# Dealing the decode steps of the wide weights out anew among the experts

## The chip, the cores and the metric

One core of a Trainium2 chip. The metric is the device time of one execution in microseconds (us). Engines: PE (TensorE, matrix products), DVE (VectorE), ACT (ScalarE), POOL (GpSimd) and SP (SyncE, which issues nearly all loads here). A difference in time is judged against repeated runs of the same kernel.

## What is computed

A windowed attention (4 x 8 heads, 576 positions) gives 2304 tokens of 512 columns. A gate sends each token to one of eight experts. Then a wide layer follows, whose weights come as 64-bit floats:

```python
for e in range(8):                        # experts: w1[e] 512 x 1024, w2[e] 1024 x 512
    h = np.maximum(x[mask_e] @ w1[e], 0)
    out[mask_e] = gate_w[mask_e, None] * (h @ w2[e])
g = np.maximum(out @ w_in, 0) ** 2        # wide layer: w_in 512 x 2048, w_out 2048 x 512
return g @ w_out
```

## The kernel before, in words

**Stages.** Attention and routing come first, then the experts one after another, the fullest first, each with a fixed number of token columns (`ROWS`: 384, 384, 352, 352, 304, 256, 256, 224), then the wide layer in nine groups of 256 tokens. Rows that do not fit an expert's columns would be done in a loop under a branch (`overflow`, line 1053), which all engines pass after expert 7.

**An expert** (line 999). The first product, s1 (line 784), goes over eight blocks `fc` of 128 hidden columns: twelve matmuls into a PSUM bank (two names, two buffers each), then a relu whose high half is written by ACT (line 793) and whose low half, the rest to 32-bit precision, by DVE (line 794). The second, s2 (line 835), goes over four blocks `d`; each takes all eight `fc` in order, with lines 844 (high weight, high relu), 845 (high weight, low relu) and 846, and ACT copies the bank to `yT` (line 847). So s2 of an expert starts with the relu halves that s1 made, in the same order.

**Expert weights.** Four quarters of w1 and four of w2 per expert, 512 KB each. `raw_w` (line 737) loads one with a DMA of SP into a staging buffer, and `split` (line 762) turns it into two 16-bit halves, the high one on ACT (line 764), the low one on DVE (line 765), in a ring `wr` of twelve buffers. The quarters of expert e+1 are loaded and split by code that stands in expert e: those of w1 after `fc` 1, 3, 5 and 7, those of w2 after each `d`. `stage` (line 748) chooses the staging buffer: the raw ring `rw` of four buffers (`raw()`, line 123), or a tile of `wi_s` that the wide weights do not yet use, by the table `SPARE` (line 51).

**Decode steps.** The wide weights have to be turned from 64-bit floats into 32-bit ones and split. This is done in 32 steps, in this order (line 939): eight `out_step` (line 900; their result is sent to device memory and fetched again late), sixteen `in_step` (line 869), which fill the eight tiles `wi_s[0..7]`, two each, and eight `out_step` whose result is kept. A step loads into a buffer of the raw ring (lines 855 to 859), decodes on DVE with three operations into the one buffer `dec` (lines 864 to 866); an `in_step` then forms four sums (lines 887 to 890). Its finish is a high half on ACT (line 895, or 911) and a low half on DVE (line 896, or 912). A call of `wide()` (line 920) finishes the step of the call before and begins the next one. Six calls stand in front of expert 0; `STEPS` (line 49) lists for each expert after which `fc` of s1 and after which `d` of s2 a call stands; three more are in `moe2` (line 1230), behind the branch.

```python
STEPS = (((2, 6), ()), ((1, 5), (1,)), ((4,), (1,)), ...        # line 49
            if fc in STEPS[e][0]:                               # line 1019
                wide()
            if d in STEPS[e][1]:                                # line 1034, in then(d), called after each d of s2
                wide()
```

The wide layer's first products are `wide1` (line 1163), from `wi_s`, its second ones `wide2` (line 1199), from `wo_s`: `wide1(0, 0)` stands ahead of s2 of expert 7, `wide1(0, 1)` behind the branch, and `wide2(0, 0)`, which reads all eight kept tiles, after it. `norm` (line 1095) prepares a group's input; the first one runs in expert 6.

**Order.** The instructions of an engine run in one line, each waiting for its inputs and for the buffer it writes. That line is not the order of the code: instructions are ordered when the program is built, with the code's order as one input, so work can stand well ahead of where it is written if its buffers are free. SP's loads are one such line.

Of the kernel before, what the change touches and what calls it, by code (L numbers as in the profile page):

```python
# [45 lines left out]
TINY, HUGE = 1e-30, 1e30  # L46
GT = 2
GW = GT * P
STEPS = (((2, 6), ()), ((1, 5), (1,)), ((4,), (1,)), ((1, 5), (1,)), ((1, 5), (1,)), ((3,), (1, 3)), ((3,), (1, 3)),
         ((1, 3, 5, 7), (1, 3)))  # L50
SPARE = ((), (4, 5, 6, 7), (4, 5, 6, 7), (4, 5, 6, 7), (4, 5, 6, 7), (6, 7), (7,), ())
KEPT = (0, 1, 8, 9, 2, 3, 10, 11)
SENT = (4, 5, 12, 13, 6, 7, 14, 15)

# [35 lines left out]
class K:  # L90
# [656 lines left out]

    def stage(self, which, e, c):

        free = SPARE[e]  # L750
        n = 4 * (which - 1) + c
        if n % 2 == 0 and e > 1 or not free or (which, e) == (1, 1):
            return self.raw()
        return self.wi_s[free[(n if e == 1 else n // 2) % len(free)]].rearrange("p k a c -> p (k a c)").bitcast(F32)[:, :1024]

# [164 lines left out]
    def wide(self, k=1):  # L920
        def store():
            while len(self.stored) > (2 if self.steps and self.steps[0][0] != self.in_step else 0):
                self.stored.pop(0)()

        for _ in range(k):
            store()
            if self.finish:
                self.finish()
                self.finish = None
            if self.steps:  # L930
                f, *a = self.steps.pop(0)
                self.finish = f(*a)
# [22 lines left out]
    def experts(self, stack):  # L955
# [20 lines left out]
        def gather(e):  # L976
            c0, c1 = blocks(e)[0][0], blocks(e)[-1][0] + 1
            nc.gpsimd.tensor_scalar(idx[:, e, c0:c1], idt[:, e, c0:c1, 0], float(N - 1), None, op0=ALU.min)
            xgs[e] = [self.gather_x(idx[:m, e, c:c + 1]) for c, m in blocks(e)]
# [19 lines left out]
        for e in range(E):  # L999
# [10 lines left out]
            for fc in range(8):  # L1010
# [6 lines left out]
                if fc % 2 == 1 and more and e > 0:  # L1017
                    w[1, e + 1, fc // 2] = self.load_w(1, e + 1, fc // 2)
                if fc in STEPS[e][0]:
                    wide()  # L1020
# [5 lines left out]
            def then(d):  # L1026
                if more:
                    w[2, e + 1, d] = self.load_w(2, e + 1, d)
                if e + 2 < E:
                    if d == 0:  # L1030
                        prep(e + 2)
                    if d == 2:
                        gather(e + 2)
                if d in STEPS[e][1]:
                    wide()
# [280 lines left out]
```

## Time and profile before

| | |
|---|---|
| median of 3 runs | 775.46 us (773.32 to 777.34) |
| the profiled execution | 774.25 us |
| its span (first to last instruction) | 772.2 us |
| PE busy / weight loads busy | 728.1 us (94%) / 559.2 us (72%) |
| DVE / ACT / POOL busy | 540.1 us (70%) / 361.2 us (47%) / 133.7 us (17%) |
| mean granted TensorE clock | 0.984 of full speed |
| DMA | 91.63 MB |

The shares are averages over stages that differ: attention fills the first 170 us or so, the experts run to 413.6 us, and the wide layer, a long stretch of matmuls, takes the rest. What the change touches lies between 180 and 437 us, and is to be read there.

### The profile page before, as it was taken

To read this page: it belongs to the slowest core of one execution; us is meant where nothing else is said; L and a number is where in the kernel's file an instruction comes from. 1 tells how busy PE (TensorE), PEld (TensorE's weight loads), DVE (VectorE), ACT (ScalarE), POOL (GpSimd) and SP (SyncE) were. 2 spreads that over 40 slices of the span, in tenths; PEclk is the share of its full clock that TensorE was granted. 3 is DMA by queue.
4 is the path that set the end of the run, shared out by engine and by line. 5 is a ranking of instruction groups with operands and counts; after the bars stand their busy time and mean duration, and the time that the engine had idled before them with its cause. 6 is when DMAs were issued, how large, how long until landed. Compare 5 with 4: busy or idle time off the path is not lost. (4 is left out here: it accounts for less than half of the span.)

```text
span 772.2 us, 18404 instructions
## 1 busy us (share of the span) xinstructions
PE 728.1 (94%) x7547; PEld 559.2 (72%) x7547; DVE 540.1 (70%) x1352; ACT 361.2 (47%) x636; POOL 133.7 (17%) x183
## 2 busy tenths in 40 slices
PE   6989999998989899899798999999999999999996
PEld 5889899787646566688698777777777777777772
DVE  5898788855879897568798774747474756566440
ACT  5878898744556574465444342423232323323220
POOL 4583421525543020000000010101010000000001
PEclk9999999899999999999899999999999999999999
DMA  9796214867897874457514000000000000000000
GB/s 336 291 388 149 67 56 120 240 177 213 286 311 231 272 252 136 152 171 249 181 57 138 3 28 2 29 1 29 2 22 8 15 15 15 15 14 15 15 14 28
DMA packets 35650, 91.63 MB, mean 119 GB/s; under 512 B 5209, under 2 KB 13547, under 8 KB 35547
## 3 DMA queue, kind: packets, MB, share of 16 engines
q1 hardware_dynamic: 29803, 75.77, 30.3%
q0 software_dynamic: 5760, 14.65, 5.7%
q8 instruction: 61, 1.00, 0.5%
q14 instruction: 26, 0.21, 0.1%
HBM read 77.54 MB, written 13.04 MB: 117 GB/s over the span
## 5 line engine op out<-in xcount | busy, mean ns | idle before, releaser
L1159 PEld LDWEIGHTS <-wi 128*128 128x128 f16 x3024 | 170.4, 98 | 6.4 <-issue 2.6
L1220 POOL DMA_INDIRECT out_dram<-o,oid x18 | 17.5, 973 | 464.5 <-ACT o L1218 464.5
L1179 ACT CAST wr<-work 128x1024 f16<-128x1024 f32 x36 | 37.6, 1045 | 123.1 <-DVE work L1178 123.1
L845 PE MATMUL ps_c<-work,wr 128*128 128x352 f16 (+5 forms) x256 | 73.8, 294 | 10.2 <-DVE work L794 9.4
L844 PE MATMUL ps_c<-work,wr 128*128 128x352 f16 (+5 forms) x256 | 73.5, 293 | 5.9 <-ACT work L793 3.2
L846 PE MATMUL ps_c<-work,wr 128*128 128x352 f16 (+5 forms) x256 | 73.9, 294 | 0.0
L305 PE MATMUL ps_a<-yT,wr 128*128 128x192 f32 (+2 forms) x288 | 64.3, 343 | 6.6 <-DMA wr<-in_q_dram 5.0
L1184 DVE TENSOR_TENSOR work<-work 128x512 f32<-128x512 f32 x18 | 12.4, 692 | 77.2 <-ACT work L1171 77.2
L1159 PE MATMUL ps_c<-work,wi 128*128 128x128 f16 x1032 | 64.9, 219 | 0.0
L1159 PE MATMUL ps_a<-work,wi 128*128 128x128 f16 x1032 | 64.7, 219 | 0.0
L317 ACT ACTIVATE pb<-pb,nm 128x192 f32<-128x192 f32 (+2 forms) x144 | 56.2, 433 | 12.4 <-DVE nm L310 11.7
L1159 PE MATMUL ps_b<-work,wi 128*128 128x128 f16 x960 | 60.1, 219 | 1.5 <-DVEq L1057 1.5
L1211 PE MATMUL ps_d<-wr 128*128 128x512 f16 x144 | 54.6, 379 | 0.1
L1212 PE MATMUL ps_d<-wr 128*128 128x512 f16 x144 | 54.6, 379 | 0.0
L1213 PE MATMUL ps_d<-wr 128*128 128x512 f16 x144 | 54.6, 379 | 0.0
L1213 PE MATMUL ps_d<-rw,wr 128*128 128x512 f16 x144 | 54.6, 379 | 0.0
L1212 PE MATMUL ps_d<-rw,wr 128*128 128x512 f16 x144 | 54.6, 379 | 0.0
L1211 PE MATMUL ps_d<-rw,wr 128*128 128x512 f16 x144 | 54.6, 379 | 0.0
L1213 PEld LDWEIGHTS <-wr 128*128 128x128 f16 x288 | 28.1, 98 | 33.9
L765 DVE SCALAR_TENSOR_TENSOR wr<-rw,wr 128x1024 f16<-128x1024 f32 x36 | 43.7, 1217 | 11.1 <-ACT wr L764 11.0
L1180 DVE TENSOR_TENSOR wr<-work,wr 128x1024 f16<-128x1024 f32 x36 | 44.0, 1221 | 10.0 <-ACT wr L1179 10.0
L305 PEld LDWEIGHTS ps_a<-yT,wr 128*128 128x128 f32 x288 | 45.1, 199 | 7.8 <-DMA yT<-in_k_dram 6.1
(248 smaller groups left out, 1693.8 us busy)
## 6 DMA issues: line engine op xcount, KB each, us to landing
rw<-in_w_dram SPq DMA_DIRECT2D x36, 512.0 KB, 5.5
wi<-in_w_dram SPq DMA_DIRECT2D x24, 512.0 KB, 5.3
rw<-in_wo_dram SPq DMA_DIRECT2D x16, 512.0 KB, 4.2
rw<-in_wi_dram SPq DMA_DIRECT2D x32, 256.0 KB, 5.2
wr<-in_q_dram SPq DMA_DIRECT2D x14, 512.0 KB, 8.0
xd<-xhl POOLq DMA_DIRECT2D x16, 256.0 KB, 4.5
yT<-in_k_dram SPq DMA_DIRECT2D x7, 576.0 KB, 10.7
rw<-in_v_dram SPq DMA_DIRECT2D x12, 325.0 KB, 5.6
```

Of the source, the lines that this page charges most:

```text
L305: nc.tensor.matmul(ps[:, s, first:hi], q[g, u, hh // 4][:, hh % 4, s if u < 4 else 0, :], self.kt[g, hh // 2][:, hh % 2, key0:key0 + hi - ...
L317: self.last_exp = nc.scalar.activation(pb[:, s, first:hi], pb[:, s, first:hi], AF.Exp, bias=nm[:, s:s + 1], scale=-1.0)
L765: self.nc.vector.scalar_tensor_tensor(t[:, 1], st, sc, t[:, 0], op0=ALU.mult, op1=ALU.subtract)
L844: nc.tensor.matmul(py, wh, hh, start=fc == 0, stop=False)
L845: nc.tensor.matmul(py, wh, hl, start=False, stop=False)
L846: self.last_mm = nc.tensor.matmul(py, wl, hh, start=False, stop=fc == 7)
L1159: self.nc.tensor.matmul(ps[:, j], w[:, kp, a, w0 * P:(w0 + 1) * P], v[:, 2 * x + kp], start=kp + b == 0, stop=kp == 1 and b == 2)
L1179: nc.scalar.copy(g[0][:, :, i], ci)
L1180: V.tensor_tensor(g[1][:, :, i], ci, g[0][:, :, i], op=ALU.subtract)
L1211: nc.tensor.matmul(py, gh, wh, start=n == 0, stop=False)
L1212: nc.tensor.matmul(py, gh, wl, start=False, stop=False)
L1213: nc.tensor.matmul(py, gl, wh, start=False, stop=n == 15)
```

## The change

The table `STEPS` is dealt out anew, and `SPARE` is replaced by a count: a tile `wi_s[k]` may stage an expert's weights as long as no more than 2k - 2 in_steps have been begun by the code so far.

```diff
-STEPS = (((2, 6), ()), ((1, 5), (1,)), ((4,), (1,)), ((1, 5), (1,)), ((1, 5), (1,)), ((3,), (1, 3)), ((3,), (1, 3)),
+STEPS = (((1, 4, 6), ()), ((1, 5), (0, 2)), ((5,), (0, 2)), ((1, 5), (0, 2)), ((3,), (0, 2)), ((), (1,)), ((), ()),
          ((1, 3, 5, 7), (1, 3)))
-SPARE = ((), (4, 5, 6, 7), (4, 5, 6, 7), (4, 5, 6, 7), (4, 5, 6, 7), (6, 7), (7,), ())
...
     def stage(self, which, e, c):

-        free = SPARE[e]
+        begun = 16 - sum(f == self.in_step for f, *_ in self.steps) if e > 0 and (which, e) != (1, 1) else 16
+        free = [k for k in range(4, 8) if begun + 2 <= 2 * k]
         n = 4 * (which - 1) + c
-        if n % 2 == 0 and e > 1 or not free or (which, e) == (1, 1):
+        if n % 2 == 0 and e > 1 or not free:
             return self.raw()
```

Calls of `wide()` in experts 0 to 7: before 2, 3, 2, 3, 3, 3, 3, 6; after 3, 4, 3, 4, 3, 1, 0, 6.

## Rows read from the trace of the kernel before

**Rows 1.** Windows, experts 1 to 6: us; PE, PEld, DVE, ACT, POOL busy; clock; DMA.

```profile
198.92:235.98 37.06, 34.60 (x220) 20.56 (x217) 29.90 (x50) 20.10 (x31) 17.09 (x23) 0.95 0.88 296
235.98:268.38 32.40, 30.36 (x218) 19.97 (x216) 30.06 (x67) 18.37 (x27) 8.04 (x7) 1.00 0.78 254
268.38:299.23 30.85, 30.26 (x218) 19.81 (x216) 27.96 (x49) 19.28 (x30) 4.35 (x3) 1.00 0.75 237
299.23:331.80 32.57, 28.09 (x211) 20.45 (x209) 20.59 (x33) 16.45 (x26) 0.00 (x0) 0.95 0.35 114
331.80:354.77 22.97, 22.13 (x211) 19.64 (x208) 18.45 (x32) 13.82 (x23) 0.00 (x0) 1.00 0.77 249
354.77:385.90 31.13, 26.22 (x224) 21.41 (x222) 24.22 (x45) 15.92 (x26) 0.00 (x0) 0.89 0.59 190
```

**Rows 2.** Waits of PE from 198.92 to 413.61: us in total, times, longest.

```profile
PE ps_c L845 <- DVE work L794: 9.4, 13, 1.6
PE ps_c L844 <- ACT work L793: 3.2, 3, 2.1
```

**Rows 3.** Timeline of PE in expert 6: start, us, instruction [idle before, releaser].

```profile
372.25 0.27 PE L844 MATMUL ps_c<-work,wr 128*128 128x256 f16 x1 [2.08 <-ACT work L793]
...
374.78 0.37 PE L845 MATMUL ps_c<-work,wr 128*128 128x256 f16 x1 [1.27 <-DVE work L794]
```

**Rows 4.** Window within expert 6, columns as in rows 1.

```profile
372.50:378.00 5.50, 4.04 (x20) 2.62 (x19) 4.43 (x10) 3.19 (x4) 0.00 (x0) 0.51 0.65 191
```

**Rows 5.** Timeline of ACT in expert 6.

```profile
370.18 1.06 ACT L764 ACTIVATE wr<-rw 128x1024 f16<-128x1024 f32 x1 [2.21 <-DMA rw<-in_w_dram]
...
371.82 0.39 ACT L793 ACTIVATE work<-ps_a 128x256 f16<-128x256 f32 x1
```

**Rows 6.** DVE's groups by line, whole span: busy us, mean ns, idle before.

```profile
L865 DVE SCALAR_TENSOR_TENSOR dec<-rw,dec 128x512 uint32<-128x512 uint32 x32 | 22.1, 689 | 0.5
...
L896 DVE SCALAR_TENSOR_TENSOR wi<-dec,wi 128x896 f16<-128x896 f32 x16 | 17.4, 1086 | 7.8 <-ACT wi L895 7.8
...
L864 DVE TENSOR_SCALAR dec<-rw 128x512 uint32<-128x512 uint32 x32 | 13.6, 424 | 15.9 <-PE ps_c L846 7.9 <-DMA rw<-in_wi_dram 5.3 <-DMA rw<-in_wo_dram 2.2
...
L912 DVE SCALAR_TENSOR_TENSOR wi<-dec,wi 128x512 f16<-128x512 f32 x8 | 5.5, 692 | 3.5 <-ACT wi L911 3.5
...
L889 DVE TENSOR_TENSOR dec<-dec 128x128 f32<-128x128 f32 x16 | 4.5, 283 | 0.0
```

**Rows 7.** Timeline of DVE: the tenth and the sixteenth finish of an in_step.

```profile
297.69 1.09 DVE L896 SCALAR_TENSOR_TENSOR wi<-dec,wi 128x896 f16<-128x896 f32 x1 [1.02 <-ACT wi L895]
...
377.74 1.09 DVE L896 SCALAR_TENSOR_TENSOR wi<-dec,wi 128x896 f16<-128x896 f32 x1 [1.07 <-ACT wi L895]
```

**Rows 8.** DMA issues of the page: count, KB each, median us to landing.

```profile
rw<-in_w_dram SPq DMA_DIRECT2D x36, 512.0 KB, 5.5
wi<-in_w_dram SPq DMA_DIRECT2D x24, 512.0 KB, 5.3
```

**Rows 9.** Timeline of DVE in expert 4.

```profile
306.26 1.22 DVE L765 SCALAR_TENSOR_TENSOR wr<-wi,wr 128x1024 f16<-128x1024 f32 x1
...
315.55 0.43 DVE L864 TENSOR_SCALAR dec<-rw 128x512 uint32<-128x512 uint32 x1 [2.16 <-DMA rw<-in_wi_dram]
...
330.76 1.23 DVE L765 SCALAR_TENSOR_TENSOR wr<-rw,wr 128x1024 f16<-128x1024 f32 x1 [8.11 <-ACT wr L764]
```

**Rows 10.** Timeline at the branch: DVE's last decode before it, PE's first matmul after it.

```profile
414.14 0.69 DVE L866 SCALAR_TENSOR_TENSOR dec<-rw,dec 128x512 uint32<-128x512 uint32 x1
...
415.44 0.66 PE L1159 MATMUL ps_b<-work,wi 128*128 128x128 f16 x9 [1.45 <-DVEq L1057]
```

**Rows 11.** Timeline behind the branch: DVE's last kept tile, PE's next two matmuls of wide2.

```profile
422.54 0.67 DVE L912 SCALAR_TENSOR_TENSOR wr<-dec,wr 128x512 f16<-128x512 f32 x1
...
426.55 0.39 PE L1212 MATMUL ps_d<-wr 128*128 128x512 f16 x1
426.77 0.38 PE L1213 MATMUL ps_d<-wr 128*128 128x512 f16 x1
```

## The prediction

> **What bounds the kernel now.** I read the busy times by expert first, then TensorE's waits, then the instructions around the longest wait. Every expert is one stage: a first product (s1), a second (s2), on PE without a break unless an input is late. [rows 1] has the stages of experts 1 to 6. The column to read is length less PE busy: 37.06 - 34.60 = 2.46 us of idle PE in expert 1, then 2.04, 0.59, 4.48, 0.84, and 31.13 - 26.22 = 4.91 in expert 6 (up to the last s2 matmul). The second column is the granted clock: 0.95, 1.00, 1.00, 0.95, 1.00, 0.89. Where it is under 1.00, PE ran at the lower of its two levels (1.2 instead of 2.4 GHz) for a part of the stage, and length x (1 - clock) bounds what that took: 1.9 us in expert 1, 1.6 in expert 4, 3.4 in expert 6. In expert 6 the clock was low during a wait of 1.27 us too [rows 3], where half of that (0.6) cost nothing, so I count 2.8 there. A stretch of that stage shows the level itself, 0.51 [rows 4].
>
> PE's waits [rows 2] say for what: s2 waits 9.4 us for line 794 (DVE's half of the relu split, the low part of ht) and 3.2 us for line 793 (ACT's half); the two groups left, 2.8 us, are s1 waiting for line 794. No wait names a weight. So in these stages PE is late only when DVE or ACT has something else in its line ahead of the relu split. In all, experts 1 to 6 lose 15.3 us idle and about 6.3 us to the clock.
>
> The worst place is expert 6: the matmul at 372.25 waited 2.08 us for ACT, the one at 374.78 another 1.27 us for DVE [rows 3]. What stood in ACT's line is in [rows 5]: a weight split of expert 7 that waited 2.21 us for its DMA, then a transpose copy, and only then the relu at 371.82.
>
> **The decode steps.** One in_step costs DVE 0.42 + 0.69 + 0.69 for the three decode operations (L865 is as long as L866), 4 x 0.28 for L887 to L890 and 1.09 for L896: 4.0 us; one out_step 0.42 + 0.69 + 0.69 + 0.69 = 2.5 us [rows 6]. The sixteen L896 tell where the in_steps really ended: 2 in expert 1, 4 in expert 2, 4 in expert 3, 2 each in experts 4, 5 and 6 ([rows 7] has the tenth and the last). That is not where their calls stand: the tenth, done at 297.69, is closed by a call in s2 of expert 4, a stage that begins only at 299.23. The order on an engine is thus not that of the code; a call bounds its step only loosely, and steps ran early wherever buffers let them.
>
> **The change part by part.** Calls made by the end of experts 0 to 7 go from 8, 11, 13, 16, 19, 22, 25, 31 to 9, 13, 16, 20, 23, 24, 24, 30. The number of instructions and of DMAs stays; a step that moves takes its loads on SP's line with it.
>
> *Out of experts 5 and 6.* Before, four in_steps end there, 4 x 4.0 = 16 us of DVE, and the first kept out_step, 2.5 us. After, only in_step 16 is begun there (15 may end there). They also stop taking buffers of the raw ring: each took one of the four between expert 7's loads. DVE was busy 24.22 of 31.13 us in expert 6 [rows 1]; without some 10 us it has half its time free. Bounds: nothing returns, if the waiting weight split of [rows 5] is all that matters, or all of 4.9 + 2.8 = 7.7 us. I take all but 1.5 us (about twice the 0.84 of expert 5, which has as many rows and runs at full clock; the norm's operations stay in expert 6): **-6.2 us**. Expert 5 itself I leave, between -0.8 and +2.1 (one ACT wait as in [rows 3]).
>
> *Into experts 0 to 4.* By the end of expert 3 the calls are 20 instead of 16, but before the change the steps were already at the tenth in_step, which is call 19's work. So really moved into experts 1 to 3 is about one in_step, and two or three into expert 4. In expert 4 DVE is idle 32.57 - 20.59 = 12.0 us, 8.11 us of it in one piece that waits for a weight split [rows 9]: three steps of 4.0 fit. Its own loss (4.5 + 1.6 = 6.1 us) comes from four weight splits in a row (the last begins at 306.26) and from a decode that waited 2.16 us for its DMA ahead of a relu split [rows 9], and both can stay; bounds -6.1 and +4.0 (a step in front of the relu split). I take 0. In experts 1 to 3 DVE is idle 7.2, 2.3 and 2.9 us. If that covers the step, the cost is 0; if the step stands before s2, it is 4.0 and a drop of the clock as in expert 1, 1.9. I take one more stall of expert 2's size: **+2.0 us**. Expert 0's third call is within that: its step needs the one decode buffer, which the steps before it hold.
>
> Here a rule speaks against the change. What the rows show is that DVE's busy share does not foretell the stalls: it is 0.93 and 0.91 in experts 2 and 3, which lose 2.6 us together, and 0.78 in expert 6, which loses 4.9 [rows 1]. The Trainium skill (Perfetto Trace Analysis, Identifying the Most-Contended Engine) takes occupancy as the measure for the Vector engine and says to relieve the engine where it is highest; by it, steps would be moved into the two fullest stages. An estimate by that page: a step of 4.0 us against idle time of which little can be used, so about 4 us instead of my 2.0, and 2 us less gain. Stalls and busy share do not go together in this trace; where the rule holds, the third rival decides.
>
> *Staging.* Which weights are staged in wide-weight tiles changes: 24 loads go through wi and 36 through rw before [rows 8]; by the new rule 4 + 4 + 4 + 4 + 1 = 17 through wi, and 43 through rw. Loads take as long either way (5.3 and 5.5 us). For experts 5 to 7 SP then has four buffers alone. One buffer turns round in 5.5 (landing) + 1.06 (ACT's split) + 1.22 (DVE's) = 7.8 us [rows 5, 8, 9], so eight loads take 2 x 7.8 = 15.6 us, under expert 5's 22.97. Cost 0, hidden under s1 and s2; without that cover it is the 2.2 us of [rows 5] again, in experts 5 and 6: bounds 0 and +4.4. In expert 4, three loads and one of expert 5 share tile 7 on SP's in-order queue; before, expert 6's four did the same. 0. POOL's queue has no part in the change.
>
> *Expert 7 and the branch.* PE waits 1.45 us at the overflow branch for DVE, which decodes kept step 7 until 414.83 [rows 10]. After, the calls before the branch reach kept step 6 only, one out_step (2.5 us) less if in_step 16 is done early, as the others were: **-1.45 us** (bounds -1.45 and 0).
>
> *After the branch.* Two kept steps are loaded and decoded there instead of one. Before, the last one was ready at 422.54 + 0.67, and wide2 starts at 426.55 [rows 11]; it reads that tile as the last of eight, after 21 matmuls 0.22 us apart, 4.6 us later. One more step, 2.5 us, fits into 426.55 + 4.6 - 423.2 = 8.0 us. 0, and +2.5 without that cover.
>
> Sum: -6.2 + 2.0 - 1.45 = -5.65 us. The profiled execution took 774.25 us (span 772.2 and 2.05 around it), 1.21 under the median of 775.46, so I apply the difference to the median: **769.8 us**, -0.7%.
>
> **The rivals.** A difference under 0.5%, 3.9 us, is about what a measurement of this kernel cannot tell from none: 771.6 to 779.3.
>
> *Nothing much moves.* Steps run ahead of their calls already, and what held ACT in expert 6 was a late weight load, of which there are now more on four buffers. Then expert 6 keeps its 7.7 us: 775.46 + 2.0 - 1.45 = 776.0. For it: [rows 5, 7]. Against: two in_steps sat in the ring between just those loads.
>
> *Expert 4 clears too.* If decode steps earlier in the line leave its relu splits free, 6.1 us more: 769.8 - 6.1 = 763.7. For it: 12 us of idle DVE there. Against: the four weight splits in a row remain.
>
> *Slower: the early experts overflow.* Place: the turn from s1 to s2 in experts 1 to 3, where DVE is busy 0.81 to 0.93. Price: a step ahead of the relu split there holds PE 4.0 us, and about 1.9 us of low clock follows. The gain to eat is 6.2 + 1.45 = 7.65, so it decides from 7.65 + 3.9 = 11.5 us on: two steps and their clock, 11.8, are just enough; with three steps and two drops, 12.0 + 3.8 = 15.8, it is 775.46 - 7.65 + 15.8 = 783.6. For it: DVE has 5.2 us free in experts 2 and 3. Against: only about one step more really goes there. [rows 9] show the form it takes: a decode at the head of DVE's line with a relu split behind it.
>
> **How the numbers follow.** Forecast 0.42, expert 4 clears too 0.14, nothing moves 0.26, slower 0.18. So faster 0.56, same 0.26, slower 0.18. The forecast's own range is 766.3 (no rest in expert 6 and no early stall, 3.5 less) to 771.6. For 8 in 10 the range runs from 762.0 (the second rival and 1.7 below) to 780.0 (all of the no-change case and the edge of the slow one); about 0.15, mostly the slow case's, is left out.
>
> **What would show it.** Right: at most two L896 after expert 4's end, 17 and 43 loads on wi and rw, expert 6 with under 2 us of PE idle and a clock above 0.97, no wait at the branch. Wrong: expert 6 still waiting on lines 793 and 794, with ACT held by a weight load (first rival), or PE idle in experts 1 to 3 above 9 us (third).

## The result and the profile after

The changed kernel takes 780.55 us (776.25 to 784.30), the kernel before, on the same chip, 775.72: a ratio of **1.0071** [1.0053, 1.0089], 5.5 us slower by the ratio (4.8 by the medians) where 5.65 us of gain were forecast, and 0.55 us above the range that was to hold 8 times in 10. Profiled, its span is 777.1 us against 772.2.

The windows of the changed kernel, experts 1 to 6, columns as in [rows 1]:

```profile
198.47:236.91 38.44, 34.79 (x219) 20.42 (x217) 29.65 (x50) 20.10 (x30) 17.17 (x24) 0.96 0.84 267
236.91:273.63 36.72, 31.59 (x218) 20.49 (x216) 33.20 (x74) 19.59 (x28) 7.40 (x7) 0.95 0.75 243
273.63:309.78 36.15, 32.42 (x219) 20.49 (x217) 29.53 (x52) 20.43 (x31) 2.81 (x3) 0.95 0.65 204
309.78:339.98 30.20, 27.65 (x211) 20.25 (x209) 25.49 (x46) 15.78 (x25) 0.00 (x0) 0.94 0.62 191
339.98:367.60 27.62, 24.20 (x211) 20.53 (x209) 16.52 (x26) 15.54 (x25) 0.00 (x0) 0.94 0.54 174
367.60:391.68 24.08, 22.89 (x224) 20.26 (x222) 16.44 (x28) 13.22 (x23) 0.00 (x0) 1.00 0.57 198
```

Read the first column against [rows 1]: +1.38, +4.32, +5.30, -2.37, +4.65, -7.05 us. The last is the gain that was forecast (24.08 - 22.89 = 1.19 us idle, clock 1.00). Stages 2 and 3 lost most beside stage 5: idle PE (length less busy) went from 2.04 and 0.59 to 5.13 and 3.73, and the granted clock from 1.00 to 0.95. Stage 5, which was to stay, lost as much: its idle went from 0.84 to 3.42.

The waits of PE over the same stretch, to set beside [rows 2]:

```profile
PE ps_c L845 <- DVE work L794: 11.1, 11, 2.1
PE ps_a L790 <- DVE work L794: 4.4, 1, 4.4
PE ps_c L844 <- ACT work L793: 2.7, 3, 1.3
PE ps_b L790 <- DVE work L794: 1.3, 2, 0.7
```

The same lines 793 and 794, with one new long wait: a first matmul of s1 that stood 4.4 us. Nothing is left at the branch, where PE had waited 1.45 us [rows 10]. The loads are 17 through `wi` and 43 through `rw`, as counted.

**Stage 2: where the 4.4 us come from.** First ACT, then DVE, then PE, of the changed kernel:

```profile
239.77 1.06 ACT L764 ACTIVATE wr<-rw 128x1024 f16<-128x1024 f32 x1 [3.37 <-DMA rw<-in_w_dram]
...
245.39 1.06 ACT L764 ACTIVATE wr<-rw 128x1024 f16<-128x1024 f32 x1 [1.99 <-DMA rw<-in_w_dram]
246.35 0.45 ACT L793 ACTIVATE work<-ps_a 128x352 f16<-128x352 f32 x1
```

```profile
234.28 1.23 DVE L765 SCALAR_TENSOR_TENSOR wr<-rw,wr 128x1024 f16<-128x1024 f32 x1 [0.23 <-ACT wr L764]
...
244.88 0.41 DVE L864 TENSOR_SCALAR dec<-rw 128x512 uint32<-128x512 uint32 x1
...
248.74 0.52 DVE L794 SCALAR_TENSOR_TENSOR work<-ps_a,work 128x352 f16<-128x352 f32 x1
...
251.71 1.09 DVE L896 SCALAR_TENSOR_TENSOR wi<-dec,wi 128x896 f16<-128x896 f32 x1 [2.21 <-ACT wi L895]
```

```profile
238.55 0.31 PE L792 MATMUL ps_a<-work,wr 128*128 128x352 f16 x1
...
249.31 0.31 PE L790 MATMUL ps_a<-work,wr 128*128 128x352 f16 x1 [4.40 <-DVE work L794]
```

The late relu belongs to the first product of s1, which was done by 238.86 (238.55 + 0.31); PE makes three more products and then needs that bank again. ACT's half stood behind two weight splits that waited 3.37 and 1.99 us for their loads, so it began at 246.35. DVE's half came only at 248.74: no instruction of DVE's line between 234.28 and 251.71 had idle time before it, so from 234.28 on DVE worked off two decode steps, weight splits and small operations of the routing (lines 686 to 706), and the relu came behind them. Both lines were late. By ACT's half alone DVE could have begun at 246.80 and PE would have waited about 2.5 us; DVE's line held it for the full 4.40. DVE had also lost time earlier to late splits. Its waits for ACT's half of a split, from 198 to 275 us, before and after:

```profile
DVE wr L765 <- ACT wr L764: 3.7, 3, 2.2
```

```profile
DVE wr L765 <- ACT wr L764: 7.3, 6, 2.3
```

Its waits of all kinds grew less: up to this relu, from 198 to 249 us, they are 9.1 us against 8.1 before. So most of what stood ahead of the relu in DVE's line was its own work. The waits of ACT for the loads, from 195 to 400 us, before and then after:

```profile
ACT wr L764 <- DMA rw<-in_w_dram: 15.5, 10, 3.3
ACT wr L764 <- DMA wi<-in_w_dram: 9.9, 7, 2.1
```

```profile
ACT wr L764 <- DMA rw<-in_w_dram: 29.0, 16, 3.9
ACT wr L764 <- DMA wi<-in_w_dram: 16.4, 7, 3.8
```

From 25.4 to 45.4 us: in the changed kernel ACT waits nearly twice as long for weights, and a relu can stand behind a waiting split in ACT's and DVE's lines.

**Stage 5: the raw ring alone.** DVE and PE of the changed kernel:

```profile
340.45 4.63 DVE L765 SCALAR_TENSOR_TENSOR wr<-rw,wr 128x1024 f16<-128x1024 f32 x4 [0.16 <-ACT wr L764]
...
356.37 1.09 DVE L896 SCALAR_TENSOR_TENSOR wi<-dec,wi 128x896 f16<-128x896 f32 x1 [1.01 <-ACT wi L895]
357.38 0.42 DVE L794 SCALAR_TENSOR_TENSOR work<-ps_b,work 128x256 f16<-128x256 f32 x1
```

```profile
355.21 0.27 PE L845 MATMUL ps_c<-work,wr 128*128 128x256 f16 x1 [1.30 <-DVE work L794]
356.66 0.27 PE L844 MATMUL ps_c<-work,wr 128*128 128x256 f16 x1 [1.07 <-ACT work L793]
357.85 0.27 PE L845 MATMUL ps_c<-work,wr 128*128 128x256 f16 x1 [0.92 <-DVE work L794]
```

Four splits in a row (4.63 us) open the stage. The loads of three quarters of w1 of expert 6 were issued at 328.14, 331.40 and 332.01, and that of the fourth at 337.09, when a decode step had left its buffer; so w1 filled all four raw buffers. Their splits need room in the ring `wr`, which the last block `d` of s2 of expert 4 (336.9 to 340.1) gives up buffer by buffer, and the first load of w2 was issued at 341.70, behind the first of these splits. ACT then waits for those too:

```profile
345.55 1.06 ACT L764 ACTIVATE wr<-rw 128x1024 f16<-128x1024 f32 x1 [1.44 <-DMA rw<-in_w_dram]
...
351.35 1.06 ACT L764 ACTIVATE wr<-rw 128x1024 f16<-128x1024 f32 x1 [1.25 <-DMA rw<-in_w_dram]
```

By the time s2 begins, the finish of an in_step (356.37) stands ahead of the last relu, and PE waits 1.30 + 1.07 + 0.92 = 3.29 us of the stage's 3.42.

### The profile page after: what moved, and what is told of

Read it like the earlier page. It is cut to its first block, busy times and chain, and to the rows that moved or that the text cites. A ratio compares the mean times of both kernels' runs of the same rounds, so it can differ in the third digit from the quotient of the medians.

```text
span 777.1 us, 18408 instructions
## 1 busy us (share of the span) xinstructions
PE 729.9 (94%) x7547; PEld 558.9 (72%) x7547; DVE 538.3 (69%) x1352; ACT 360.9 (46%) x636; POOL 132.4 (17%) x183
## 5 line engine op out<-in xcount | busy, mean ns | idle before, releaser
L765 DVE SCALAR_TENSOR_TENSOR wr<-rw,wr 128x1024 f16<-128x1024 f32 x43 | 52.1, 1221 | 15.9 <-ACT wr L764 15.8
L764 ACT ACTIVATE wr<-rw 128x1024 f16<-128x1024 f32 x43 | 44.9, 1055 | 29.2 <-DMA rw<-in_w_dram 29.0
L1213 PEld LDWEIGHTS <-wr 128*128 128x128 f16 x288 | 28.2, 98 | 33.9
L309 DVE CUSTOM_DVE_ANT_0 pb<-ps_a,bias 128x192 f32<-128x192 f32 (+2 forms) x144 | 44.2, 327 | 9.7 <-PE ps_a L304 7.9
```

Source lines behind the costliest of these rows:

```text
L309: self.last_ttr = nc.vector.tensor_tensor_reduce(out=pb[:, s, first:hi], in0=ps[:, s, first:hi], in1=self.bias[:, hh, first - lo:192], sca ...
L764: self.nc.scalar.activation(t[:, 0], st, AF.Copy, scale=sc)
L765: self.nc.vector.scalar_tensor_tensor(t[:, 1], st, sc, t[:, 0], op0=ALU.mult, op1=ALU.subtract)
L1213: nc.tensor.matmul(py, gl, wh, start=False, stop=n == 15)
```

## The experiments

Two theories, which do not exclude each other. **A: late loads in an in-order line.** Weight loads come late, for want of staging buffers (tile 7 shared by expert 4's loads, the raw ring alone for experts 5 to 7) and behind the moved steps' loads; their splits wait at the head of ACT's and DVE's lines, and the relu behind them. **B: DVE is full.** The moved decode work itself fills DVE in experts 1 to 3. Ratios are to the kernel before, run beside each kernel on the same chip; it took 775.72 us beside the change, 770.66 beside 1 to 4, 774.60 beside 5 to 8 and 770.80 beside 9 to 12, so kernels are compared by ratio. In the profiled executions expert 0 ends at 195.1, 199.3 and 196.1 us in the mean of these three groups, so most of that difference lies ahead of the stages. The stage lengths of the profiled executions, experts 1 to 6, in us:

| kernel | ratio [95%] | 1 | 2 | 3 | 4 | 5 | 6 |
|---|---|---|---|---|---|---|---|
| before | 1 | 37.1 | 32.4 | 30.9 | 32.6 | 23.0 | 31.1 |
| after | 1.0071 [1.0053, 1.0089] | 38.4 | 36.7 | 36.2 | 30.2 | 27.6 | 24.1 |
| after, again (x5) | 1.0063 [1.0037, 1.0089] | 37.2 | 36.3 | 33.9 | 32.5 | 28.6 | 25.9 |
| long staging (x1) | 1.0011 [0.9988, 1.0034] | 39.8 | 34.6 | 31.8 | 30.9 | 23.4 | 24.5 |
| staging rule alone (x2) | 0.9973 [0.9947, 0.9999] | 34.7 | 34.4 | 29.9 | 30.7 | 23.0 | 26.8 |
| late move only (x3) | 0.9942 [0.9919, 0.9965] | 37.2 | 34.3 | 29.9 | 28.4 | 28.0 | 23.5 |
| late move, long staging (x7) | 0.9908 [0.9873, 0.9944] | 37.8 | 35.6 | 29.9 | 26.7 | 25.7 | 24.5 |

**1. Weights staged in the wide tiles for longer** (`x1_steps_long_staging`), the changed kernel with

```diff
-        free = [k for k in range(4, 8) if begun + 2 <= 2 * k]
+        free = [k for k in range(4, 8) if begun <= 2 * k + 1]
```

> The new dealing of the steps, but the expert weights stay in wide-weight tiles as long as the step that fills a tile is not yet finished by the code (begun <= 2k + 1 instead of begun <= 2k - 2): four weights each of experts 3 to 5 and three of expert 6, in more than the one tile 7. Of the loss of the changed kernel, stage 2 is 4.3 us longer than before, stage 3 5.3, stage 5 4.7, stage 6 is 7.1 shorter. Theory A (late weight loads in ACT's line, because tile 7 and the raw ring serve alone): stages 3 and 5 come back by at least 3 us each, stage 2 stays; ratio to before 0.993 to 1.000. Theory B (the moved decodes fill DVE ahead of the relu splits): nothing comes back, ratio 1.005 to 1.009.

Measured: 771.62 us, 1.0011 [0.9988, 1.0034]; six tenths of a per cent below the change. Stages 3 and 5 of this kernel:

```profile
268.46:300.25 31.79, 30.39 (x218) 19.85 (x216) 27.21 (x50) 17.79 (x27) 3.42 (x3) 1.00 0.73 230
331.16:354.51 23.35, 22.21 (x211) 19.67 (x208) 15.81 (x25) 13.76 (x23) 0.00 (x0) 1.00 0.68 222
```

Stage 5 is back at its length of before, 1.14 us idle at full clock: its loss was staging, not decode steps, of which it has the same. Stages 1 and 2 are not cleared. The ratio is just above the range of A, and the profiled execution (766.72 us) was this kernel's shortest, so its stages are on the low side.

**2. The new staging rule with the old table** (`x2_staging_rule_alone`)

```diff
-STEPS = (((1, 4, 6), ()), ((1, 5), (0, 2)), ((5,), (0, 2)), ((1, 5), (0, 2)), ((3,), (0, 2)), ((), (1,)), ((), ()),
+STEPS = (((2, 6), ()), ((1, 5), (1,)), ((4,), (1,)), ((1, 5), (1,)), ((1, 5), (1,)), ((3,), (1, 3)), ((3,), (1, 3)),
```

> The old dealing of the steps with the new staging rule, which then gives almost the tiles of the old table. Both theories: stages 1 to 6 as before within 1 us each, ratio 0.997 to 1.003. If it is slower by more than 0.4%, the rule itself costs and the dealing is innocent.

Measured: 768.25 us, 0.9973 [0.9947, 0.9999]. The rule alone costs nothing: with the old table, in_steps begin later, so the rule leaves the tiles to the weights for longer (23 loads through `wi` against 17). What hurts is the count meeting the early table. Stages 1, 2 and 6 came out 2.4 us shorter, 2.0 longer and 4.3 shorter than before, with the same calls, where 1 us was expected: so much can a stage differ between single executions.

**3. Only the steps of experts 5 and 6 moved, into experts 3 and 4** (`x3_late_move_only`), the changed kernel with

```diff
-STEPS = (((1, 4, 6), ()), ((1, 5), (0, 2)), ((5,), (0, 2)), ((1, 5), (0, 2)), ((3,), (0, 2)), ((), (1,)), ((), ()),
+STEPS = (((2, 6), ()), ((1, 5), (1,)), ((4,), (1,)), ((1, 5), (0, 2)), ((1, 3, 5), (0, 2)), ((3,), (1,)), ((), ()),
```

> Experts 0 to 2 as before, the steps of expert 6 put into experts 3 and 4 (calls by the end of experts 0 to 6: 8, 11, 13, 17, 22, 24, 24), new staging rule. Theory A and B alike: stages 1 and 2 as before (37 and 32.4 us), stage 6 about 24 as in the changed kernel. Theory A: stage 5 still about 27 us, since its weights come through the raw ring alone, ratio 0.995 to 1.000. Theory B: stage 5 about 23, as DVE is not fuller there than before, and stage 4 longer by 2 to 4; ratio 0.991 to 0.998.

Measured: 766.50 us, 0.9942 [0.9919, 0.9965], clearly faster than before, and 1.3% under the change. Stages 5 and 6:

```profile
325.52:353.54 28.02, 22.98 (x211) 19.68 (x209) 21.35 (x37) 18.11 (x28) 0.00 (x0) 1.00 0.64 207
353.54:377.04 23.50, 22.89 (x225) 20.23 (x222) 16.58 (x28) 13.22 (x23) 0.00 (x0) 1.00 0.61 203
```

Expert 6 is as clear as in the changed kernel, so its gain needs no other calls in experts 0 to 2 than the old ones; stage 5, with 18 loads in all through `wi` under the short staging, is 28 us as A expected (B: 23). The ratio is below the range of A and within that of B, but stage 4 was shorter (28.4 us) where B expected it longer.

**4. Weight splits behind the newest relu** (`x4_splits_behind_relu`), the changed kernel with the two relu halves remembered in `s1`, and in `load_w`

```diff
-        return self.split(self.raw_w(which, e, c), W1SC if which == 1 else W2SC)
+        st = self.raw_w(which, e, c)
+        with self.tc.issue_after(self.relu_act.ins), self.tc.issue_after(self.relu_dve.ins):
+            return self.split(st, W1SC if which == 1 else W2SC)
```

> The changed kernel, with each weight split kept behind the last relu that stands ahead of it in the code, on ACT and on DVE, so that a split that waits for its load can't stand ahead of an earlier relu. Theory A: the waits of s1 and s2 for lines 793 and 794 fall to less than half in stages 2, 3 and 5 (from 16 us there to under 8), unless the splits then come too late and PE waits for weights instead (new waits naming line 764 or 765); ratio 0.985 to 1.000. Theory B: the waits stay, ratio 1.003 to 1.010.

Measured: 766.20 us, 0.9941 [0.9913, 0.9970]: 1.2 to 1.3% off the change with no step or load moved. Stages 2 and 5:

```profile
234.76:268.62 33.86, 31.62 (x218) 20.59 (x216) 32.71 (x74) 19.00 (x28) 5.88 (x5) 0.95 0.78 256
333.36:355.21 21.85, 21.85 (x210) 19.68 (x208) 14.44 (x23) 13.05 (x21) 0.00 (x0) 1.00 0.58 172
```

Stage 5 has no idle PE at all, DVE in stage 2 is as busy as before the edit (32.71 us against 33.20), and the stage 2.9 us shorter. Idle PE in stages 2, 3 and 5 fell from 12.3 to 2.5 us. The order in the line is thus a condition of much of the loss. Not all of it goes: stages 1 and 4 became longer (41.8 and 34.2 us, with 6.7 and 5.0 us idle), and in stage 2 one wait is left (line numbers are two higher in this kernel):

```profile
PE ps_a L792 <- DVE work L796: 2.2, 1, 2.2
```

It is for the relu of the first product again, which now stands behind two decode steps and the routing in DVE's line, with no split between. This part is B, DVE's own work alone: half of the 4.4 us stays without any split.

**5. The changed kernel once more** (`x5_changed_again`), no edit.

> The changed kernel itself, beside the runs below on one chip, so that its stages are compared with theirs under the same conditions. Both theories: stages 3 and 5 longer than 34 and 26 us, ratio 1.004 to 1.010.

Measured: 779.12 us, 1.0063 [1.0037, 1.0089]. Single stages scatter by 2 us and more between executions (stage 3: 33.87 instead of 36.15), so a stage is read from several profiles; stage 5 stays slow (28.56). This profiled execution (782.37 us) was the longest of its kernel.

**6. Long staging for the loads of expert 4 alone** (`x6_long_staging_expert4`)

```diff
-        free = [k for k in range(4, 8) if begun + 2 <= 2 * k]
+        free = [k for k in range(4, 8) if begun + 2 <= 2 * k or e == 4 and begun <= 2 * k + 1]
```

> The changed kernel, with the longer staging (begun <= 2k + 1) for the weights of expert 4 alone, which stage 3 loads: tiles 4 to 7 serve instead of 6 and three times 7. Experts 5 to 7 stay on the raw ring. Theory A with tile 7 as the place: stage 3 falls from about 36 to under 33 us, stage 5 stays at 26 or more, ratio about 1.000 to 1.004. If stage 3 stays at 34 or more, its loss is from the moved steps and not from tile 7 (theory B there).

Measured: 778.20 us, 1.0054 [1.0025, 1.0083], within the interval of the change. Stage 3 took 32.2 us, under both profiles of the change, but no gain shows in the time, which is above the range of A: tile 7 alone is a small part at most.

**7. Late move and long staging together** (`x7_late_move_long_staging`): the edits of 1 and 3.

> Steps as in x3 (experts 0 to 2 as before the change, expert 6 emptied into 3 and 4), with the longer staging. Theory A: stage 5 falls from 28.0 to about 23 us as well, stages 1, 2 and 6 as in x3; ratio 0.986 to 0.993. Theory B: as x3, 0.992 to 0.997.

Measured: 767.46 us, **0.9908** [0.9873, 0.9944]: faster than both kernels. It splits the whole difference into steps from one kernel to the next: late move with long staging (7 against before), -0.92%; the steps moved early as well (1 against 7), +1.03%; staging given up early (the change against 1), +0.60%. Of 775.5 us that is -7.1 + 8.0 + 4.6 = +5.5 us; each step has an interval of some 0.3 to 0.4% either way. The split depends on the order of the steps: with the short staging, the early move costs 1.29% (the change against 3). Stage 5 fell to 25.7 us and not to 23, with DVE busy 20.42 us in it against 15.81 in 1, so its rest is not staging.

**8. The kernel before, with its splits behind the relu** (`x8_before_splits_behind_relu`): the edit of 4 on the kernel before.

> The kernel before, with each weight split kept behind the last relu ahead of it in the code, on ACT and DVE. Theory A: the waits in expert 6 of before (2.1 us for ACT, 1.9 for DVE) came from splits that stood ahead and waited for loads; stage 6 falls from 31 to under 28 us and the waits for lines 793 and 794 in experts 1 to 6 from 15 us to under 9; ratio 0.985 to 0.996. Theory B: DVE is as full in stage 6, ratio 0.996 to 1.004.

Measured: 769.12 us, 0.9942 [0.9919, 0.9965]. The order cost the kernel before about 0.6% too, and with it gone both tables give the same ratio, 0.9941 and 0.9942, within intervals of 0.3%: under this order the change loses no time to the kernel before. By stages that is a balance: the change is still longer in stages 2 and 4 (33.9 and 34.2 us in 4, 30.0 and 30.6 here) and shorter in stage 6 (23.4 against 30.2). Stage 6 was expected under 28 us here; it kept 4.9 us idle, 2.5 of them a wait for the norm.

**9. Long staging for experts 5 to 7 alone** (`x9_long_staging_experts56`)

```diff
-        free = [k for k in range(4, 8) if begun + 2 <= 2 * k]
+        free = [k for k in range(4, 8) if begun + 2 <= 2 * k or e > 4 and begun <= 2 * k + 1]
```

> The changed kernel with the longer staging for the weights of experts 5 and 6 alone (tiles 6 and 7 in place of the raw ring), expert 4's as the change has them. Theory A with the raw ring as the place: stage 5 falls from 28 to about 23.5 us, stage 3 stays at 34 or more; ratio 0.998 to 1.003. Theory B: stage 5 stays above 26, ratio 1.004 to 1.009.

Measured: 773.61 us, 1.0016 [0.9986, 1.0046]. Stages 3 and 5:

```profile
273.69:310.60 36.91, 33.49 (x218) 20.87 (x216) 28.70 (x52) 19.56 (x29) 3.87 (x3) 0.91 0.67 214
338.03:360.98 22.95, 22.05 (x211) 19.66 (x209) 15.80 (x25) 13.75 (x23) 0.00 (x0) 1.00 0.66 225
```

Stage 5 is cleared and stage 3 is not: six loads put back into the tiles buy nearly all that long staging buys in 1.

**10. Light decodes** (`x10_light_decode`), the changed kernel with

```diff
-        V.scalar_tensor_tensor(t, w[:, :, 1], 0xC0000000, t, op0=ALU.bitwise_and, op1=ALU.bitwise_or)
-        V.scalar_tensor_tensor(t, w[:, :, 0], 29, t, op0=ALU.logical_shift_right, op1=ALU.bitwise_or)
+        if len(pieces) == 1:
+            V.scalar_tensor_tensor(t, w[:, :, 1], 0xC0000000, t, op0=ALU.bitwise_and, op1=ALU.bitwise_or)
+            V.scalar_tensor_tensor(t, w[:, :, 0], 29, t, op0=ALU.logical_shift_right, op1=ALU.bitwise_or)
```

> The changed kernel with one of the three decode operations in every in_step (the other two, 0.69 us each, are left out, so the wide weights hold other values): 16 x 1.38 = 22 us less for DVE, the loads as they are. Theory B (DVE too full): the idle time of PE in stages 1 to 3 falls by half or more, from about 11 us to under 6; ratio 0.993 to 1.000. Theory A (late loads ahead of the relu): it falls by less than 3 us, ratio 1.001 to 1.007.

Measured: 764.17 us, 0.9879 [0.9837, 0.9920]. Stages 2 and 3, and ACT's waits for the loads from 195 to 400 us:

```profile
236.52:273.17 36.65, 31.88 (x219) 20.70 (x217) 31.02 (x72) 22.64 (x32) 5.14 (x6) 0.95 0.82 273
273.17:303.66 30.49, 30.33 (x218) 19.84 (x216) 25.05 (x46) 20.46 (x30) 3.81 (x3) 1.00 0.73 244
```

```profile
ACT wr L764 <- DMA wi<-in_w_dram: 17.3, 9, 3.7
ACT wr L764 <- DMA rw<-in_w_dram: 10.2, 8, 2.7
```

A third of each in_step's work on DVE gone, and 1.9% of the time with it: B is not false. But a faster decode also frees its raw buffer sooner, and the waits for `rw` fell from 29.0 to 10.2 us, so this run cannot hold A and B apart, and its ratio lies below the ranges of both. Idle PE in stages 1 to 3 fell to 9.2 us, where B expected under 6. Stage 2 is against B as the whole account: less work, the same length (36.65), and a matmul of s1 that still waits 3.90 us for line 794.

**11. Half of each in_step's loads** (`x11_half_step_loads`), the changed kernel with

```diff
-        f = self.wide_load(self.wi, [part(0), part(1)])
+        rows, c0, n, _ = part(0)
+        f = self.wide_load(self.wi, [(rows, c0, 2 * n, lambda st, k: st.rearrange("p (b c) -> p b c", b=4)[:, 0:2])])
```

and the half that was loaded decoded twice, with as much work on DVE as before.

> The changed kernel with half of each in_step's load (its second part is left out and the first decoded twice, so the wide weights hold other values): 16 loads of 256 KB fewer on SP and on the DMA engines, DVE's work as it is. Theory A: the weight loads land earlier, ACT waits less for them in stages 1 to 5, PE's idle time in stages 1 to 3 falls by 3 us or more, ratio 0.996 to 1.002. Theory B: nothing of it, ratio 1.004 to 1.009.

Measured: 766.89 us, 0.9915 [0.9883, 0.9948]. ACT's waits for the loads, from 195 to 400 us:

```profile
ACT wr L764 <- DMA rw<-in_w_dram: 26.6, 18, 3.4
ACT wr L764 <- DMA wi<-in_w_dram: 8.3, 6, 3.0
```

The time fell by 1.5%, mostly in stages 4 and 5 (27.2 and 24.3 us); idle PE in stages 1 to 3 stayed at 10.5 us, as in the second profile of the change (12.5 in the first). The long wait in stage 2 halved (2.17 us). The ratio is below the ranges of both theories, and the idle time of stages 1 to 3, which A expected to fall by 3 us or more, did so by 2 at most. So loads matter as well, and neither 10 nor 11 clears the early stages alone.

**12. The edits of 7 with the splits behind the relu** (`x12_late_move_long_staging_behind_relu`).

> x7 (late move, longer staging) with the weight splits kept behind the relu as in x4 and x8. Theory A: what is left in stages 2 and 5 of x7 (about 3 us of idle PE each) goes; ratio 0.980 to 0.989. Against it: in x8 the splits came late in stage 6 and PE waited for the norm; if that holds here, about as x7, 0.988 to 0.994.

Measured: 766.26 us, 0.9930 [0.9901, 0.9958], no better than 7. The gains do not add: with the splits behind the relu, the kernel before, the change and this third table all come to 0.993 or 0.994. So under this order neither the early move's loss nor the late move's gain shows in the time. PE's longest wait in expert 6 is then 2.7 us, for ACT's work on the norm (line 1105 of this kernel), which stands behind two splits that waited for their loads (0.94 and 0.27 us).

## Why the prediction was wrong

**Out of experts 5 and 6** stood in kind. -6.2 us was forecast for expert 6, -7.05 measured, by the signs named: idle 1.19 us, clock 1.00, no L896 in it (2, 4, 5, 4, 1, 0 in stages 1 to 6). The closeness is in part luck of the executions read: with the old steps, the kernel of 2 took 26.8 us there and not 31.1, and the second profile of the change 25.9, with 3.05 us idle; from the means of these pairs the gain is about 4 us. The sum of the late gains, -7.65 us with the branch, is near the -7.1 of experiment 7, but not by the same stages: there stage 6 gave 6.7 and stage 4 another 5.8 us (32.6 to 26.7), while stages 2 and 5 lost 3.2 and 2.7.

**The branch** gave its 1.45 us, and nothing new waits behind it: the next wait of PE, at the first matmul of wide2 (419.66), is 0.15 us.

**Expert 4**, forecast 0 between -6.1 and +4.0, came out at -2.37 and, in the second profile, -0.03.

**Into experts 0 to 4: the first step that failed.** "+2.0 us", one stall of expert 2's size, measured +11.0 in stages 1 to 3 (+9.0 as the mean of two profiles), and +1.03%, 8.0 us, by times alone (1 against 7). The count was right, one in_step more in these stages. The price was wrong: I charged one stall of 2.0 us, with one step of 4.0 us ahead of one relu as the bound. But the early steps also made weight splits late, and a late split holds ACT's and DVE's whole lines, the relu included. I had seen that form in [rows 5] and used it for expert 6 alone. ACT's waits for the loads show it with the staging held equal, from 195 to 400 us, first in 7, with the old calls in experts 0 to 2, then in 1, with the new:

```profile
ACT wr L764 <- DMA rw<-in_w_dram: 14.1, 10, 2.7
ACT wr L764 <- DMA wi<-in_w_dram: 9.5, 6, 3.5
```

```profile
ACT wr L764 <- DMA rw<-in_w_dram: 23.2, 13, 3.3
ACT wr L764 <- DMA wi<-in_w_dram: 19.2, 11, 4.5
```

From 23.6 to 42.4 us: nearly all of the growth seen in the change comes with the early steps, and not with the staging. The stage figures are less sure than the times. The one execution of before is on the short side in stage 2 (32.4 us); the kernels of 2, 3 and 7, with its calls up to expert 2, took 34.3 to 35.6 us there.

**Staging: the second step that failed.** "Cost 0, hidden under s1 and s2" was 4.6 us (2.3 us either way), about the +4.4 I gave as the upper bound. Its argument, "eight loads take 2 x 7.8 = 15.6 us, under expert 5's 22.97" treats a raw buffer as free after its split. But a split needs room in `wr`, which comes only as s2 of the expert before passes. The four buffers were full of w1 until stage 4 ended, and the 7.8 us began there for w2. Before, the tiles had held a part of those loads. It is the same loss that shows in expert 5, +4.65 against my bounds of -0.8 and +2.1.

**The rivals.** The third, the early experts overflowing (783.6 us, chance 0.18), came nearest, with its place right and its sign met (PE idle in stages 1 to 3 of 12.5 and 10.5 us, above 9). Its price, whole steps ahead of the relu, is a part of the mechanism (the 2.2 us left in 4) and not the whole of it. I gave the first rival's clause, more late loads on four buffers, to expert 6; it was expert 5 that paid.

The fullest stages, 2 and 3, lost 4.3 and 5.3 us. The Trainium skill (Perfetto Trace Analysis, Identifying the Most-Contended Engine) takes the engine of highest occupancy as the one to optimise first. Read as a caution against filling DVE where it is fullest, it agrees with this trace in sign; the estimate of 4 us made from it was about half of what was measured. Experiment 4 shows what occupancy leaves out: DVE as busy in stage 2, PE 2.9 us less held.

The four raw buffers full behind `wr` are a case of what the Trainium skill (Perfetto Trace Analysis, Optimization Strategy) names as a possible cause of gaps that repeat, too little buffer room for the next tile; 1 and 9 agree, with 4 to 5 us in stage 5.

**What stays open** is how the 8 us of the early move divide between DVE's own work and the late loads: 10 and 11 each take part of it, and each changes the raw ring besides. A longer raw ring under the early table, which would part the two, was not run. Shown is that the early steps make the loads late (1 against 7), that the order of splits and relus decides what this costs in the time (4 and 8), that DVE's work holds a relu of stage 2 without any split (4), that tile 7 alone is little (6), and that with the old calls in experts 0 to 2 the loss does not arise (3 and 7).

## What to carry to other kernels

Where an engine's line holds both prefetch work and the operation that the next product needs, the price of moved work is not its own time alone: ask which prefetch it makes late and what stands behind that prefetch. Count a staging buffer from its load to the moment its consumer has room to write, not to the end of a turn at full speed. And when a change frees one stage, move the work into the stages with idle time alone: here the late half of the move was worth 0.9%, and the early half took more than that back.

## What the runs showed of the hardware

A load's time is not fixed. A weight load of 512 KB through `rw` took 5.5 us to land [rows 8] and between 4.9 and 6.4 us in the experiments with all of the steps' loads for which the profile gives it; in experiment 11, where the in_steps load half as much, it took 4.3 us (medians). I had taken it as the same wherever the steps' loads stand. I had also not expected how much two executions of one kernel differ by stage while their times agree within 0.5%: 2.3 us in stage 3 and 1.9 us in stage 6 between the two profiles of the change.
